# One core's two-resolution attention with a routed MLP: wider pooled-score matmuls, x tiles left uncleared, v sums in three steps, and a new order of all steps

## The chip, the cores and the metric

The kernel runs on one core of a Trainium2 chip. Its time is the device time of one execution in microseconds; the median of three runs is 284.74 us. The core's engines work side by side, each through its own queue in program order: TensorE (PE) multiplies matrices, VectorE (DVE), ScalarE (ACT) and GpSimd (POOL) do elementwise work, and SyncE (SP) issues most of the transfers. Only PE, DVE and ACT reach PSUM, where matmul results lie.

## The reference

Eight batches (`B = 8`), eight heads, 576 tokens, head size 64. Two attentions are added, and the result goes through a routed MLP:

```python
q_d = q.reshape(B, H, Sd, factor, D).mean(axis=3)      # factor 4: 144 pooled tokens; k and v alike
out_d = sm_attn(q_d, k_d, v_d)
out_up = np.repeat(out_d, factor, axis=2)
mask = np.abs(pos[:, None] - pos[None, :]) < factor     # a band of 7 keys
out_local = softmax(where(mask, scale * q @ k.T, -1e9)) @ v
x = (out_up + out_local) as (B, S, H * D)
scores = np.einsum('bsd,d->bs', x, w_gate)
for b in range(B):
    top_idx = the 128 best tokens by scores[b]
    out[b, top_idx] = x[b, top_idx] + sigmoid(scores[b, top_idx])[:, None] * (relu(x[b, top_idx] @ w1) @ w2)
```

## The kernel before, in words

The kernel writes down some 930 **steps**, each a few instructions of one engine with the tiles it reads and writes. `Plan.order` then emits them in an order that comes from a table of numbers, `PLACES`: of all steps that could go next, the one with the smallest place does. So the table fixes, for each engine, in which order its instructions stand; at run time each engine goes through its queue and waits for what an instruction needs.

Every batch b runs through the same stages, and batches overlap:

- **Loads** (SP): `T` holds q and k of the batch, transposed (2.3 MB, two tiles in turn); `raw` the four token phases of v (1.15 MB, one tile); `vw` the windows of v in three pieces. Weights come in eight pieces through `hid`; ACT and DVE split each into a high and a low fp16 half (L409, L412).
- **Pooling**: for batch 0 DVE sums q and k (L484); for the others POOL does it in two halves of the heads, each by `one` (L492, `half<-T`) and `two` (L496, `dT<-half`). POOL sums v (`add`, L450 and L452, three additions in one step) and spreads the 16 tokens beyond the 128th (`spread`, L458).
- **Coarse attention** (`coarse`): pooled scores in two groups u (L529, the 16 tokens beyond the 128th in L536), row maxima on DVE (L547), exponentials on ACT, copies for the last tokens on POOL (L570, L576, `erx`), transposes on PE (L513, L591 to L593), products with v (L603, L611, L618, L625), division on DVE (`dens`, L636 to L647). The result `ods` is raised to full length: for batches 0 and 1 by matmuls (L678, `raise_by_products`, with a POOL step `apart`, L666), for the others by 12 DMAs from `ods` and `pd` into the tile `x` (`raise_by_copies`: four steps `up` of two DMAs, one step `up_last` of three, one `down`).
- **Local attention** (`local`), three groups of two, two and one tiles: scores (mask L756, q times k L768), maximum and difference on DVE (`top`, L779 and L780), exponential on ACT, transposes (L513) and products (L814) on PE, division on DVE (`norm`, L824 to L826), the sum into `x` (`add`, L836; on DVE for batches 0 and 7, on POOL for the others), and the score of each token on DVE (`dot`, L843). Then SP stores `x` (L864, five DMAs for a batch).
- **Route**: token scores are joined (L880), transposed (L896), compared (L906), counted (L916) and turned into a one-hot matrix (ACT L935) that picks 128 tokens (`pick`, PE L943; `found`, DVE L952). POOL gathers their rows from the output (L958).
- **MoE**: transposes of the gathered rows (L981), up (L1002 to L1004) and down (L1024 to L1026) matmuls in fp16 halves, low halves on DVE (L988, L1014), the sum (`join`, DVE L1032) and a scatter by POOL (L1037).

At the start POOL clears tiles (`set_up`, L366), among them both `x` tiles of 128 by 2560 floats.

Of the kernel before, what the change touches and what calls it, by code (L numbers as in the profile page):

```python
# [21 lines left out]
P = 128  # L22
# [9 lines left out]
UL = 2  # L32
FAST = (0, 7)
SUMS = (0,)
LIFT = (0,1)
TU = [list(range(u, min(u + UL, NT))) for u in range(0, NT, UL)]
XS = 16.0
# [2 lines left out]

EARLY = {
    "load": 0.48, "pool": -1.58, "coarse": -1.53, "raise": 3.84, "local": -0.18,
    "sum": 1.35, "lift": 0.5, "route": -8.17, "moe": 3.14, "weights": 3.02,
}


PLACES = """
# [33 lines left out]
"""  # L81


# [171 lines left out]
def tile_multires_attention_moe(ctx: ExitStack, tc: tile.TileContext, qk, vw, vp, cs, w_gate, w1, w2, outs):  # L255
# [97 lines left out]
    def pref(kind, b, more=0.0):  # L353
        return b + EARLY[kind] + more
# [7 lines left out]
    )  # L362

    def set_up():
        for t in (*qzs, first, *xs):
            pool.memset(t, 0.0)  # L366
        pool.memset(ones, 1.0)
        for t in vds:
            pool.memset(t[:, :, D:], 1.0)

    step("POOL", 6000, set_up, (), ("zero",), -9)

    def set_up2():
        dve.tensor_copy(identb, ident)
# [63 lines left out]
    def load_v(b):  # L438
        raw = Buf("raw")
        step(  # L440
            "SP", 0, lambda: sp.dma_start(
            out=raw.at.rearrange("p (r s) h d -> p r (s h d)", r=2), in_=vp[b].rearrange("r p s h d -> p r (s h d)"),
        ), (), (raw,), pref("load", b, 0.35),
            moves=[(400, 3070)],
        )
        vd = vd_[b] = Buf("vd")

        def add():
            o = vd.at[:, :, :D]
            pool.tensor_tensor(out=o, in0=raw.at[:, 0], in1=raw.at[:, 1], op=ALU.add)  # L450
            for r in range(2, FACTOR):
                pool.tensor_tensor(out=o, in0=o, in1=raw.at[:, r], op=ALU.add)  # L452

        step("POOL", 4180, add, (raw, "zero"), (vd,), pref("pool", b, 0.2))
        vr = vr_[b] = Buf("vr")

        def spread():
            pool.tensor_tensor(  # L458
                out=vr.at, in0=vd.at[:, H : H + 1, :].broadcast_to([P, HH, D1]),
                in1=bk.unsqueeze(2).broadcast_to([P, HH, D1]), op=ALU.mult,  # L460
            )

        step("POOL", 610, spread, (vd, "cst"), (vr,), pref("pool", b, 0.3))
        vwin[b] = []
        for i, tiles in enumerate(TU):
            t = Buf(f"vw{i}")
            vwin[b].append(t)

            def go(t=t, tiles=tiles):
                sp.dma_start(out=t.at, in_=vw[b][:, 2 * tiles[0] : 2 * tiles[-1] + 2])  # L470

            step("SP", 0, go, (), (t,), pref("load", b, 0.4 + 0.1 * i), moves=[(350, 815 * len(tiles))])
# [44 lines left out]
    def coarse(b):  # L517
        dT, qz, vd, vr = qkdT[b], qz_[b], vd_[b], vr_[b]
        ed, er, erx, ptr = Buf("ed"), Buf("er"), Buf("erx"), Buf("ptr")
        for u in range(2):  # L520
# [3 lines left out]
            def scores(u=u, s=s):  # L524
                for i in range(2):
                    hp = 2 * u + i
                    for x in range(2):
                        for a in range(2):
                            pe.matmul(  # L529
                                s.at[64 * x : 64 * x + 64, a, SD * i : SD * (i + 1)],  # L530
                                lhsT=dT.at[64 * a : 64 * a + 64, hp, 0, 64 * x : 64 * x + 64],
                                rhs=dT.at[64 * a : 64 * a + 64, hp, 1, :], start=True, stop=True,
                            )
                if u:
                    for hp in range(HP):
                        pe.matmul(  # L536
# [63 lines left out]
        def products():  # L600
# [20 lines left out]
                        start=False, stop=True, skip_group_check=True,  # L621
                    )
            for a in range(2):
                for x in range(2):
                    pe.matmul(  # L625
                        od.at[64 * x : 64 * x + 64, a, : HH * D1],
                        lhsT=ptr.at[64 * a : 64 * a + 64, 0, 64 * x : 64 * x + 64],
                        rhs=vr.at[64 * a : 64 * a + 64].rearrange("p h d -> p (h d)"), start=False, stop=True,
                        skip_group_check=True,
                    )  # L630

        step("PE", 2280, products, (ptd, ptr, vd, vr), (od,), pr, 70)
        op = lambda: od.at[:, :, : (HH + 1) * D1].rearrange("p a (h d) -> p a h d", d=D1)
# [102 lines left out]
    def local(b):  # L736
        T, x, sc = qkT[b], xb[b], Buf("sc")
        scs[b] = sc
        for i, tiles in enumerate(TU):
# [37 lines left out]
            def top(s=s, mx=mx, ex=ex, ns=ns, ng=ng):  # L777
# [4 lines left out]
                    in1=mx.at[:, :, :ng].unsqueeze(3).broadcast_to([P, 2, ng, KW]), op=ALU.subtract,  # L782
                )

            step("DVE", 250 + 1070 * ns, top, (), (s, mx, ex), pr, 80)
            step(
                "ACT", 100 + 430 * ns,
                lambda ex=ex, ng=ng: act.activation(ex.at[:, :ng], ex.at[:, :ng], AF.Exp, scale=scale),  # L788
                (), (ex,), pr, 100,
            )  # L790
            ps, pt = Buf("pair", "local"), Buf("pt")
            pr = pref("local", b, 0.3 * i + 0.05)

# [343 lines left out]
```

## Time and profile before

| | us |
|---|---|
| median of three runs (284.70 to 285.36) | 284.74 |
| the profiled execution | 282.83 |
| its span, first to last instruction | 281.0 |
| PE busy | 230.4 |
| DVE busy | 211.6 |
| POOL busy | 164.0 |
| ACT busy | 127.9 |

Busy time counts the stretches in which an engine had work in it, so overlapping matmuls count once. The granted TensorE clock is 0.953 of full over the span.

### The profile page before, as it was taken

What the parts mean: (1) busy time and instruction counts of PE and PEld (TensorE: products, weight loads), DVE (VectorE), ACT (ScalarE), POOL (GpSimd) and SP (SyncE); (2) the same over time, 40 slices, a digit from 0 to 9 for tenths busy, and PEclk for the clock granted to TensorE, in tenths of its full rate; (3) what the DMA queues carried; (4) which work ended last, traced back from release to release, by engine and by line L of the source; (5) the groups of instructions that cost most, each with busy time, mean ns of one, the idle gap of its engine ahead of it and who ended that gap; (6) DMA issues with size and microseconds to landing.
All of it is one profiled execution on the core that took longest, in us unless ns stands there. A gap on an engine that the chain in (4) does not pass through costs nothing.

```text
span 281.0 us, 11847 instructions
## 1 busy us (share of the span) xinstructions
PE 230.4 (82%) x5160; PEld 172.9 (62%) x5160; DVE 211.6 (75%) x507; ACT 127.9 (46%) x264; POOL 164.0 (58%) x177
## 2 busy tenths in 40 slices
PE   0668767698685876689898999898999989999992
PEld 0455455555564765666686677655875776886670
DVE  4975595979999698398798897798997899862311
ACT  0476588536582475144533366236715436232010
POOL 8253999794999876909936797595633321111201
PEclk9989979979779899799999999999999999999998
DMA  7999996909899999887597879978878871521100
GB/s 277 418 354 418 413 395 228 340 8 303 249 354 290 385 355 335 231 179 185 162 394 246 251 214 326 272 178 236 184 171 229 212 186 54 145 67 37 40 37 37
DMA packets 23229, 66.00 MB, mean 235 GB/s; under 512 B 3346, under 2 KB 3346, under 8 KB 23178
## 3 DMA queue, kind: packets, MB, share of 16 engines
q1 hardware_dynamic: 21898, 61.06, 68.1%
q0 software_dynamic: 1280, 4.20, 4.5%
q8 instruction: 40, 0.66, 0.9%
q14 instruction: 11, 0.09, 0.1%
HBM read 47.02 MB, written 11.73 MB: 209 GB/s over the span
## 4 chain that ended last, share of the span: by engine, by line
PE 41%; DVE 16%; issue 15%; DMA 11%; POOL 10%; ACT 6%; SPq 1%; POOLq 0%; DVEq 0%; ACTq 0%
DMA xe<-out_dram,idx 5%; PE ps L814 4%; PE ps L1002 4%; PE ps L1004 3%; PE ps L1003 3%; PE ps L1024 3%; PE ps L513 3%; PE ps L1026 3%; PE ps L1025 3%; DVE t L843 3%; DMA T<-in_qk_dram 2%; POOL half L492 2%; DMA raw<-in_vp_dram 2%; PE ps L768 2%; PE ps L611 2%
## 5 line engine op out<-in xcount | busy, mean ns | idle before, releaser
L836 POOL TENSOR_TENSOR x<-x,t 128x512 f32<-128x512 f32 x30 | 39.2, 1315 | 19.9 <-DVE t L826 12.4
L1002 PE MATMUL ps<-xeh,w1h 128*128 128x128 f16 x256 | 45.5, 221 | 2.1 <-DVE t L843 1.5
L1003 PE MATMUL ps<-xel,w1h 128*128 128x128 f16 x256 | 45.3, 221 | 0.0
L1004 PE MATMUL ps<-xeh,w1l 128*128 128x128 f16 x256 | 45.3, 221 | 0.0
L814 PE MATMUL ps<-vw,pt 64*64 64x65 f32 x1280 | 29.0, 227 | 9.0 <-issue 7.5
L814 PEld LDWEIGHTS ps<-vw,pt 64*64 64x64 f32 x1280 | 23.9, 137 | 17.1 <-issue 11.4
L492 POOL TENSOR_TENSOR half<-T 128x1152 f32<-128x1152 f32 x14 | 29.5, 2105 | 2.6 <-DMA T<-in_qk_dram 2.3
L843 DVE SCALAR_TENSOR_TENSOR t<-x,ps 128x512 f32<-128x512 f32 x40 | 26.9, 682 | 5.1 <-PE ps L1026 1.6
L768 PE MATMUL ps<-T 64*58 64x64 f32 (+1 forms) x1280 | 26.5, 228 | 4.4 <-issue 4.4
L768 PEld LDWEIGHTS ps<-T 64*58 64x58 f32 (+1 forms) x1280 | 25.5, 138 | 6.6 <-issue 5.4
L788 ACT ACTIVATE ex<-ex 128x1024 f32<-128x1024 f32 (+1 forms) x24 | 21.9, 915 | 15.3 <-DVE ex L780 15.1
L826 DVE TENSOR_TENSOR t<-ps,den 128x512 f32<-128x512 f32 x40 | 27.7, 691 | 1.5
L779 DVE TENSOR_REDUCE mx<-ps 128x16 f32<-128x1024 f32 (+1 forms) x24 | 25.0, 1040 | 3.4 <-PE ps L768 1.9
L1003 PEld LDWEIGHTS <-w1h 128*128 128x128 f16 x256 | 25.3, 99 | 2.7 <-issue 2.0
L1002 PEld LDWEIGHTS <-w1h 128*128 128x128 f16 x256 | 25.2, 99 | 2.6 <-issue 0.7
L906 DVE SCALAR_TENSOR_TENSOR beat<-ps,scp,first 128x640 bf16<-128x640 f32 (+4 forms) x40 | 22.6, 613 | 5.6 <-PE ps L896 5.1
L1024 PE MATMUL ps<-w2h,hid 128*128 128x512 f16 x64 | 24.3, 380 | 1.9 <-DVE t L843 1.3
L800 ACT COPY pt<-ps 128x1024 f32<-128x1024 f32 (+1 forms) x24 | 20.9, 878 | 10.7 <-PE ps L513 10.3
L780 DVE TENSOR_TENSOR ex<-ps,mx 128x1024 f32<-128x1024 f32 (+1 forms) x24 | 25.1, 1047 | 0.8
L1004 PEld LDWEIGHTS <-w1l 128*128 128x128 f16 x256 | 25.3, 99 | 0.1
L1026 PE MATMUL ps<-w2h,hid 128*128 128x512 f16 x64 | 24.2, 379 | 0.0
L1025 PE MATMUL ps<-w2l,hid 128*128 128x512 f16 x64 | 24.2, 379 | 0.0
(113 smaller groups left out, 494.5 us busy)
## 6 DMA issues: line engine op xcount, KB each, us to landing
T<-in_qk_dram SPq DMA_DIRECT2D x7, 2304.0 KB
raw<-in_vp_dram SPq DMA_DIRECT2D x8, 1152.0 KB
vw<-in_vw_dram SPq DMA_DIRECT2D x16, 520.0 KB
out_dram<-x SPq DMA_DIRECT2D x14, 480.0 KB
x<-ods SPq DMA_DIRECT2D x48, 120.0 KB
hid<-in_moe_w_dram SPq DMA_DIRECT2D x8, 512.0 KB
T<-in_qk_dram SPq DMA_DIRECT2D x4, 576.0 KB
vw<-in_vw_dram SPq DMA_DIRECT2D x8, 260.0 KB
```

The source lines that it names most:

```text
L492: pool.tensor_tensor(out=hv.at, in0=e2[..., 0], in1=e2[..., 1], op=ALU.add)
L768: pe.matmul(s.at[64 * e : 64 * e + qn, a, c : c + KW], lhsT=T.at[64 * a : 64 * a + 64, hp, 0, q0s[blk] : q0s[blk] + qn], rhs=T.at[64 * a : ...
L814: pe.matmul(o.at[64 * e : 64 * e + 64, a, D1 * hp : D1 * (hp + 1)], lhsT=pt.at[64 * a : 64 * a + 64, e, HP * n + hp, :], rhs=vl.at[64 * a ...
L826: dve.tensor_tensor(out=t.at.rearrange("p (g a d) -> p a g d", a=2, d=D), in0=ov[:, :, :, 0:D], in1=den.at.unsqueeze(3).broadcast_to([P, 2 ...
L836: (dve if last else pool).tensor_tensor(out=x.at[:, j], in0=x.at[:, j], in1=t.at, op=ALU.add)
L843: dve.scalar_tensor_tensor(out=t.at, in0=x.at[:, j], scalar=1.0, in1=wg, op0=ALU.mult, op1=ALU.mult, accum_out=sc.at[:, j : j + 1],)
L1002: pe.matmul(o, lhsT=w1h[:, c, fs], rhs=xeh.at[:, c, :], start=c == 0, stop=False)
L1003: pe.matmul(o, lhsT=w1h[:, c, fs], rhs=xel.at[:, c, :], start=False, stop=False)
L1004: pe.matmul(o, lhsT=w1l[:, c, fs], rhs=xeh.at[:, c, :], start=False, stop=c == NC - 1)
L1024: pe.matmul(py.at, lhsT=hid.at[:, 0, f, :], rhs=w2h[:, f, :], start=f == 0, stop=False)
L1025: pe.matmul(py.at, lhsT=hid.at[:, 0, f, :], rhs=w2l[:, f, :], start=False, stop=False)
L1026: pe.matmul(py.at, lhsT=hid.at[:, 1, f, :], rhs=w2h[:, f, :], start=False, stop=f == NF - 1)
```

## The change

Four edits. The pooled scores and the products of the last 16 tokens run with all 128 queries as one stationary operand of 64 by 128 instead of two of 64 by 64, so there are half as many of these matmuls with as many moving columns each. The `x` tiles are no longer cleared. The three additions of v become three steps, which the order may part. `PLACES` is a new table for the 950 steps. (A second form of the local exponentials is added for batches in `EXPS`, which is empty: no step uses it. The costs written beside the steps are the planner's.)

```diff
-        for t in (*qzs, first, *xs):
+        for t in (*qzs, first):
             pool.memset(t, 0.0)
...
-        def add():
-            o = vd.at[:, :, :D]
-            pool.tensor_tensor(out=o, in0=raw.at[:, 0], in1=raw.at[:, 1], op=ALU.add)
-            for r in range(2, FACTOR):
-                pool.tensor_tensor(out=o, in0=o, in1=raw.at[:, r], op=ALU.add)
-
-        step("POOL", 4180, add, (raw, "zero"), (vd,), pref("pool", b, 0.2))
+        for r in range(1, FACTOR):
+            def add(r=r):
+                o = vd.at[:, :, :D]
+                pool.tensor_tensor(out=o, in0=o if r > 1 else raw.at[:, 0], in1=raw.at[:, r], op=ALU.add)
+
+            step("POOL", 1400, add, (raw, "zero"), (vd,), pref("pool", b, 0.2 + 0.03 * r))
...
-                    for x in range(2):
-                        for a in range(2):
-                            pe.matmul(
-                                s.at[64 * x : 64 * x + 64, a, SD * i : SD * (i + 1)],
-                                lhsT=dT.at[64 * a : 64 * a + 64, hp, 0, 64 * x : 64 * x + 64],
-                                rhs=dT.at[64 * a : 64 * a + 64, hp, 1, :], start=True, stop=True,
-                            )
+                    for a in range(2):
+                        pe.matmul(
+                            s.at[:, a, SD * i : SD * (i + 1)], lhsT=dT.at[64 * a : 64 * a + 64, hp, 0, :P],
+                            rhs=dT.at[64 * a : 64 * a + 64, hp, 1, :], start=True, stop=True,
+                        )
...
             for a in range(2):
-                for x in range(2):
-                    pe.matmul(
-                        od.at[64 * x : 64 * x + 64, a, : HH * D1],
-                        lhsT=ptr.at[64 * a : 64 * a + 64, 0, 64 * x : 64 * x + 64],
-                        rhs=vr.at[64 * a : 64 * a + 64].rearrange("p h d -> p (h d)"), start=False, stop=True,
-                        skip_group_check=True,
-                    )
+                pe.matmul(
+                    od.at[:, a, : HH * D1], lhsT=ptr.at[64 * a : 64 * a + 64, 0, :],
+                    rhs=vr.at[64 * a : 64 * a + 64].rearrange("p h d -> p (h d)"), start=False, stop=True,
+                    skip_group_check=True,
+                )
...
-    0 1 10 12 18 49 50 2 3 4 5 6 25 33 7 8 9 11 37 46 15 52 59 51 88 173 63 98 185 177 207 248 190 231 244 256 287 317
+    0 1 9 11 18 48 53 2 3 5 4 6 23 28 30 36 7 10 8 12 56 131 14 54 55 59 81 129 130 155 230 136 158 207 213 265 325
```

The table moves steps on every engine. Three places matter below. In these rows the line numbers are those of the respective kernel, and the number behind a name is that of the buffer. POOL, from the step `apart` of batch 0 on (`t<-odr`), before (`T_78`, `vd_88`, `vr_90` belong to batch 1, `T_77` to batch 2):

```order
L666 TENSOR_TENSOR t_118<-odr_103,cst 128x512
L492 TENSOR_TENSOR half_79<-T_78 128x1152
L496 TENSOR_TENSOR dT_80<-half_79 128x576
L450 TENSOR_TENSOR vd_88<-raw_86 128x9x64
L452 TENSOR_TENSOR vd_88<-vd_88,raw_86 128x9x64 x2
L492 TENSOR_TENSOR half_79<-T_78 128x1152
L496 TENSOR_TENSOR dT_80<-half_79 128x576
L458 TENSOR_TENSOR vr_90<-vd_88,cst 128x260
L492 TENSOR_TENSOR half_79<-T_77 128x1152
```

and the same place after:

```order
L662 TENSOR_TENSOR t_119<-odr_103,cst 128x512
L492 TENSOR_TENSOR half_79<-T_78 128x1152
L496 TENSOR_TENSOR dT_80<-half_79 128x576
L492 TENSOR_TENSOR half_79<-T_78 128x1152
L496 TENSOR_TENSOR dT_80<-half_79 128x576
L452 TENSOR_TENSOR vd_88<-raw_86 128x9x64
L452 TENSOR_TENSOR vd_88<-vd_88,raw_86 128x9x64 x2
L458 TENSOR_TENSOR vr_90<-vd_88,cst 128x260
L492 TENSOR_TENSOR half_79<-T_77 128x1152
```

The second half of batch 1's pooled q and k now comes ahead of its v sums instead of behind them. DVE between `dens` of batch 1 (which ends with the first row, `odr_104`) and `dens` of batch 2 (which begins with `dend_105`), before:

```order
L647 SCALAR_TENSOR_TENSOR odr_104<-ps_64,dend_106,odr_104 128x64
L836 TENSOR_TENSOR x_123<-x_123,t_119 128x512
L843 SCALAR_TENSOR_TENSOR t_119,sc_125<-x_123,ps_66 128x512
L779 TENSOR_REDUCE mx_107<-ps_63 128x16
L780 TENSOR_TENSOR ex_110<-ps_63,mx_107 128x2x8x64
L836 TENSOR_TENSOR x_123<-x_123,t_117 128x512
L843 SCALAR_TENSOR_TENSOR t_117,sc_125<-x_123,ps_66 128x512
L636 TENSOR_SCALAR dend_105<-ps_65 128x10
```

and after:

```order
L775 TENSOR_REDUCE mx_107<-ps_63 128x16
L776 TENSOR_TENSOR ex_110<-ps_63,mx_107 128x2x8x64
L837 TENSOR_SCALAR den_121<-ps_65 128x8
L838 RECIPROCAL den_121<-den_121 128x8
L839 TENSOR_TENSOR t_117<-ps_65,den_121 128x2x4x64
L849 TENSOR_TENSOR x_123<-x_123,t_116 128x512
L856 SCALAR_TENSOR_TENSOR t_116,sc_125<-x_123,ps_66 128x512
L775 TENSOR_REDUCE mx_108<-ps_63 128x16
L776 TENSOR_TENSOR ex_111<-ps_63,mx_108 128x2x8x64
L632 TENSOR_SCALAR dend_105<-ps_64 128x10
```

A third division of batch 1 (`den_121`) and the second `top` of batch 2 (`mx_108`, `ex_111`) now stand ahead of `dens` of batch 2. SP near the end, where `x_123` is batch 6 and `x_124` batch 7, before:

```order
L707 DMA x_124<-ods_102 60x1x512 x8
L470 DMA vw_85<-in_vw_dram 128x520
L707 DMA x_124<-ods_102 48x1x512
L707 DMA x_124<-pd_157 12x1x512
L707 DMA x_124<-pd_157 56x1x512
L864 DMA out_dram<-x_123 48x5x512
L864 DMA out_dram<-x_123 10x5x512
L864 DMA out_dram<-x_123 48x5x512
L864 DMA out_dram<-x_123 6x5x512
L864 DMA out_dram<-x_123 4x4x512
```

and after:

```order
L703 DMA x_124<-ods_102 60x1x512 x2
L877 DMA out_dram<-x_123 48x5x512
L877 DMA out_dram<-x_123 10x5x512
L877 DMA out_dram<-x_123 48x5x512
L877 DMA out_dram<-x_123 6x5x512
L877 DMA out_dram<-x_123 4x4x512
L703 DMA x_124<-ods_102 48x1x512
L703 DMA x_124<-pd_157 12x1x512
L703 DMA x_124<-pd_157 56x1x512
L703 DMA x_124<-ods_102 60x1x512 x2
```

The last five copies into batch 7's `x` have moved behind the five stores of batch 6.

## Rows read from the trace of the kernel before

**Rows 1.** Page, part 1: busy us (share of span) xinstructions of each engine.

```profile
PE 230.4 (82%) x5160; PEld 172.9 (62%) x5160; DVE 211.6 (75%) x507; ACT 127.9 (46%) x264; POOL 164.0 (58%) x177
```

**Rows 2.** Windows: stretch and length, busy us (instructions) by engine, granted clock, DMA share, GB/s.

```profile
0.00:45.00 45.00, 28.03 (x739) 20.48 (x741) 31.39 (x50) 25.18 (x47) 29.90 (x31) 0.92 0.93 359
45.00:100.00 55.00, 41.99 (x1104) 31.29 (x1104) 46.42 (x106) 30.57 (x63) 45.45 (x43) 0.88 0.84 283
...
130.00:200.00 70.00, 64.34 (x1545) 48.45 (x1536) 59.12 (x162) 32.31 (x73) 50.14 (x56) 1.00 0.82 249
200.00:275.00 75.00, 71.87 (x1250) 53.81 (x1248) 50.69 (x135) 25.47 (x51) 17.63 (x29) 1.00 0.46 118
```

**Rows 3.** Timeline of PE: start, us, engine, line, operation, tiles, tile shape, count.

```profile
60.50 0.67 PE L625 MATMUL ps<-vr,ptr 64*64 64x260 f32 x8
...
63.22 0.72 PE L529 MATMUL ps<-dT 64*64 64x144 f32 x16
...
65.29 0.72 PE L513 MATMUL ps<-cst,ex 64*128 64x64 f32 x16 [0.66 <-ACT pt L800]
...
68.01 0.70 PE L814 MATMUL ps<-vw,pt 64*64 64x65 f32 x32
```

**Rows 4.** Timeline of POOL, the start; in brackets idle time before and its releaser.

```profile
1.59 4.68 POOL L366 MEMSET x<- 128x2560 f32 x2
...
12.31 1.40 POOL L450 TENSOR_TENSOR vd<-raw 128x576 f32<-128x576 f32 x1 [5.92 <-DMA raw<-in_vp_dram]
```

**Rows 5.** Timeline of POOL, 26 to 47 us.

```profile
26.04 1.95 POOL L666 TENSOR_TENSOR t<-odr,cst 128x512 f32<-128x512 f32 x1 [4.66 <-DVE odr L647]
...
32.72 2.72 POOL L452 TENSOR_TENSOR vd<-vd,raw 128x576 f32<-128x576 f32 x2
...
37.58 1.14 POOL L496 TENSOR_TENSOR dT<-half 128x576 f32<-128x576 f32 x1
...
39.27 2.11 POOL L492 TENSOR_TENSOR half<-T 128x1152 f32<-128x1152 f32 x1
...
46.41 0.29 POOL L576 COPY erx<-ed 128x128 f32<-128x128 f32 x1
```

**Rows 6.** Timeline of DVE and PE, waits between 30 and 62 us.

```profile
32.19 0.76 DVE L547 TENSOR_REDUCE mxd<-ps 128x4 f32<-128x576 f32 x1 [3.02 <-PE ps L529]
...
55.80 0.30 PE L591 MATMUL ps<-cst,erx 128*128 128x128 f32 x1 [2.71 <-DVE t L843]
...
61.24 0.17 DVE L636 TENSOR_SCALAR dend<-ps 128x10 f32<-128x10 f32 x1 [1.78 <-PE ps L625]
```

**Rows 7.** Groups of DVE by form: count, busy us, mean ns, idle before.

```profile
L826 DVE TENSOR_TENSOR t<-ps,den 128x512 f32<-128x512 f32 x40 | 27.7, 691 | 1.5
L843 DVE SCALAR_TENSOR_TENSOR t<-x,ps 128x512 f32<-128x512 f32 x40 | 26.9, 682 | 5.1 <-PE ps L1026 1.6 <-ACT hid L1011 0.7 <-ACT xeh L985 0.6
L780 DVE TENSOR_TENSOR ex<-ps,mx 128x1024 f32<-128x1024 f32 x16 | 19.6, 1225 | 0.5
L779 DVE TENSOR_REDUCE mx<-ps 128x16 f32<-128x1024 f32 x16 | 19.5, 1219 | 1.7 <-ACT er L561 0.9 <-PE ps L768 0.8
L836 DVE TENSOR_TENSOR x<-x,t 128x512 f32<-128x512 f32 x10 | 7.7, 767 | 0.0
L412 DVE SCALAR_TENSOR_TENSOR w1l<-hid,w1h 128x1024 f16<-128x1024 f32 x4 | 4.9, 1217 | 0.0
```

**Rows 8.** Chain that ended last: batch 0's gather, start and us until landing.

```profile
82.58 12.65 DMA xe<-out_dram,idx
```

**Rows 9.** Chain (a copy into x) and timelines of SP, DVE, PE, late program.

```profile
129.76 4.75 DMA x<-ods
...
201.80 6.53 SPq L864 DMA_DIRECT2D out_dram<-x  x5
...
245.81 0.17 DVE L880 TENSOR_TENSOR scp<-sc,cst 128x5 f32<-128x5 f32 x1
...
254.04 0.27 PE L943 MATMUL ps<-va,oh 128*128 128x5 bf16 x5
```

More of the change, by code (lines that the diff above doesn't have):

```diff
@@ L34 @@
 SUMS = (0,)
+EXPS = ()
 LIFT = (0,1)
@@ L42 @@
     "load": 0.48, "pool": -1.58, "coarse": -1.53, "raise": 3.84, "local": -0.18,
-    "sum": 1.35, "lift": 0.5, "route": -8.17, "moe": 3.14, "weights": 3.02,
+    "sum": 1.35, "lift": .5, "route": -8.17, "moe": 3.14, "weights": 3.02,
 }
 PLACES = """
[33 rows of a table removed]
[33 rows of a table added]
 """
@@ L369, in set_up @@
             pool.memset(t[:, :, D:], 1.0)
-    step("POOL", 6000, set_up, (), ("zero",), -9)
+    step("POOL", 1500, set_up, (), ("zero",), -9)
     def set_up2():
@@ L461, in spread @@
             )
-        step("POOL", 610, spread, (vd, "cst"), (vr,), pref("pool", b, 0.3))
+        step("POOL", 610, spread, (vd, "cst"), (vr,), pref("pool", b, 0.32))
         vwin[b] = []
@@ L783, in top, with peak, exps @@
                 )
[L785 to L790, printed above, removed]
+            def peak(s=s, mx=mx, ns=ns, ng=ng):
+                sv = s.at[:, :, : 256 * ns].rearrange("p a (g c) -> p a g c", c=KW)
+                dve.tensor_reduce(out=mx.at[:, :, :ng], in_=sv, axis=AX.X, op=ALU.max)
+            def exps(s=s, mx=mx, ex=ex, ng=ng):
+                act.activation(mx.at[:, :, :ng], mx.at[:, :, :ng], AF.Copy, scale=-scale)
+                for a in range(2):
+                    for g in range(ng):
+                        act.activation(
+                            ex.at[:, g, KW * a : KW * (a + 1)], s.at[:, a, KW * g : KW * (g + 1)], AF.Exp,
+                            bias=mx.at[:, a, g : g + 1], scale=scale,
+                        )
+            if b in EXPS:
+                step("DVE", 130 + 530 * ns, peak, (), (s, mx), pr, 80)
+                step("ACT", 200 + 1650 * ns, exps, (), (s, mx, ex), pr, 100)
+            else:
+                step("DVE", 250 + 1070 * ns, top, (), (s, mx, ex), pr, 80)
+                step(
+                    "ACT", 100 + 430 * ns,
+                    lambda ex=ex, ng=ng: act.activation(ex.at[:, :ng], ex.at[:, :ng], AF.Exp, scale=scale),
+                    (), (ex,), pr, 100,
+                )
             ps, pt = Buf("pair", "local"), Buf("pt")
```

64 rows, old and new, of the table PLACES are left out of this document.

## The prediction

> **What bounds the kernel now.** I read the page's busy shares first: PE 82%, DVE 75% [rows 1]. Such a share is a mean over stages, so I took the table of windows next [rows 2]. In it the program has two halves. From 130 to 200 us PE is busy 64.3 of 70 us, from 200 to 275 us 71.9 of 75: there PE sets the pace, and no order of steps can win much. Up to 100 us it is busy 28.0 of 45 and 42.0 of 55 us: 30 us idle. DVE is idle 13.6 us of the first 45 and 8.6 of the next 55. So what a new order can win lies in the first 100 us: work that fills those holes no longer has to be done later. Third I read the timelines of POOL, DVE and PE there for what ends the holes. From 26 us on POOL works through the pooling of batches 1 and 2 [rows 5], DVE waits 3.02 us for pooled scores that need it, and before `dens` of batch 2 DVE waits 1.78 us for the products while PE had waited 2.71 us for DVE [rows 6]: engines that wait on each other in turn, with none full.
>
> **The x tiles left uncleared** take 4.68 us of POOL away [rows 4]. Behind them POOL waits 5.92 us for `raw`, which is on its way since the start, so the v sums begin at 12.31 us as before. Value 0; the cover is that transfer, and were it gone the edit would be worth the 4.68 us.
>
> **The wider matmuls.** A pooled-score group was 16 records of 64x64 with 144 columns in 0.72 us, the products of the last tokens 8 records with 260 columns in 0.67 us [rows 3]. Each gets half the records, twice as wide. The nearest rows for what width costs: 16 records of 64x128 with 64 columns take 0.72 us, 32 of 64x64 with 65 columns 0.70 us [rows 3]. Half as many, twice as wide: the same time. So I take 0 for PE. The end below zero is that a record costs the same whatever its width: half of 0.72 for the 16 groups and half of 0.67 for the 8 is 5.8 + 2.7 = 8.5 us at most, and less by the fixed latency in each; I put 4.6 (some 0.23 and 0.12 us a group). Above zero I see nothing, since the 64x128 row already pays for the width. The Trainium skill (TensorEngine Tiling (Array Packing), Instruction Overhead) states about 60 cycles of overhead for each matmul on trn2, the same latency for 1 column as for 60. By that, 160 records fewer at 2.4 GHz would be an estimate of 4 us less on PE. The trace disagrees so far: 32 records in 0.70 us leave 22 ns for each, work included [rows 3]. It is a rival below.
>
> **The v sums as three steps** are the same instructions (two take 2.72 us [rows 5]); by themselves 0. They let POOL turn to something else between two sums, up to 2.7 us sooner.
>
> **The new order.** POOL first: from `apart` of batch 0, which nothing moves (26.04 + 1.95 = 28.0 us), batch 1's two halves now follow at once, 2 x (2.11 + 1.14) = 6.5 us, so its pooled q and k are complete at 34.5 us instead of 37.58 + 1.14 = 38.7 [rows 5]: 4.2 us sooner. Its v sums end 0.6 us later than the old second half did, at about 39.3 with the spread, and still ahead of the `erx` copies, which stood at 46.41 and now stand one addition (1.1 us) sooner. Batch 1's scores, maxima and exponentials so come into the DVE hole of 3.02 us and the ones after it.
>
> DVE second, the term that carries the forecast. I compared the sets of steps ahead of `dens` of batch 2. Nothing has left; seven steps have come: three divisions of batch 1, 3 x 0.69 = 2.1 us; the second `top` of batch 2, 1.22 + 1.23 = 2.4; one weight half, 1.2; one `add` and one `dot` of batch 0, 0.8 + 0.7 [rows 7]. That is 7.2 us. They fit: up to 45 us alone DVE has 13.6 us of holes [rows 2].
> When does `dens` of batch 2 come? It began at 61.24 [rows 6]. POOL now has a half, its sum and another half of batch 3 ahead of batch 2's `erx` copies, 2.11 + 1.14 + 2.11 = 5.4 us [rows 5]. Those copies had been done by about 53 us (46.41, 0.7 for both copies, three sums 4.1, spread and copies 1.6), while PE took them at 55.80, held by DVE [rows 6]. So 2.8 us of the 5.4 were slack, and 2.6 are late; 1.1 us of that comes back from the addition that moved behind batch 1's copies. Delay 0 to 2.6 us, I take 1.2. The lead is 7.2 - 1.2 = **6.0 us**, bounds 4.6 and 7.2.
>
> Does PE follow? Ahead of the products of batch 2 it has three more product groups of 0.70 us [rows 3], two score groups, a transposition, and one lift in another's place, about 4 us; it was idle 13.0 us between 45 and 100 [rows 2], so it can.
> Is the lead kept? Up to `pick` of batch 3 (in the middle of the stretch from 130 us on) both programs have the same amount of DVE work ahead, to within half a microsecond, and the same of PE; only which differs (three MoE steps and a count of batch 4 in place of scores of batch 5). From there PE sets the pace in either. So a lead there reaches the end.
> At the end, after `pick` of batch 7 at 254.04 [rows 9], four down steps fewer are left than before, but they are done ahead of it on a full PE: 0, at best 2.6 us.
>
> **Sum.** Profiled execution 282.83 (span 281.0 and 1.8 around it): 282.8 - 0 - 0 - 6.0 = 276.8. The median of the runs lies 1.9 above the profiled execution, so in its terms 284.7 - 6.0 = **278.7**.
>
> **Rivals.**
> *Given back at the first gather.* Batch 0's gather took 12.65 us until its rows were there [rows 8], with transfers all around it. Its `found` has the moved steps ahead of it, so it comes no sooner; but up to the first MoE step of DVE both orders have nearly the same work, so between the two DVE now has some 7 us less to do. If the gather takes as long again, DVE and PE stand still for what they had won, and 0 to 1.5 us stay: 283.2 to 284.7, I say 284.0. For it: the row. Against: SP issues batch 4's `T` sooner now, since its tile is free when the local scores of batch 2 are through, and those stand further ahead.
> *Records cost, not width.* PE shorter by 4.6 us in all; on the path lie the groups behind 130 us, five of 16 and three of 8, 5 x 0.23 + 3 x 0.12 = 1.5 us, up to all 4.6: 278.7 - 4.6 to 278.7 - 1.5, 274.1 to 277.2.
> *The other side: batch 7's copies.* SP now issues batch 6's stores ahead of the last five copies into batch 7's `x`. The stores wait for POOL's last `add` of batch 6 (1.3 us), take 6.53 us to issue, the five copies at no more than a store's 1.3 us each 4 to 6.5 (I take 4), the landing 4.75 [rows 9]: 16.6 us. From the division that feeds that `add` to the `add` of batch 7 that needs the copies DVE has about 19 us of steps; these two `add` and `dot` pairs are its last ahead of the joined score (245.81 before [rows 9]). So 2.4 us of slack: from there every microsecond is paid in full, since 35 us of dependent work follow. If the stores wait for free slots as long again as they take to issue (6.5 us) and the copies likewise (4), the end is 8 us late and eats the lead: 284.7 - 6.0 + 8.1 = 286.8.
> *The order does not do what it says*: the steps pulled ahead wait in turn for PE, which runs at 0.88 to 0.92 of its clock there [rows 2], and a third of the lead stays: 282.5.
>
> **How the numbers follow.** Forecast 278.7 (277.5 to 281): 0.50. Given back: 0.17, half of it within 0.3%. Records: 0.12. Copies late: 0.13. Order empty: 0.08. Faster by over 0.3%, about what a measurement can tell from no change (below 283.9): 0.50 + 0.12 + 0.08 + 0.07 = 0.77; within: 0.10; slower: 0.13. The range 274.0 to 286.0 leaves out the upper end of the copies and the lower end of the records, less than 0.2.
>
> **What would show it.** No MEMSET of `x`, and POOL's first v sum still at about 12.3 us behind a longer wait for `raw`. A score group of 8 records still near 0.7 us. The second `two` of batch 1 ending at 34 to 35 us; `dens` of batch 2 at 61 to 64 with 4 us or more less idle time on DVE up to there; the joined score of batch 7 near 240. I am wrong if DVE idles between `found` of batch 0 and its first MoE step, if SP sits long at the stores of batch 6, or if score groups shrink to 0.5 us.

## The result: 1.3% slower, and the profile after

The changed kernel's runs have a median of 288.95 us (288.41 to 293.31), those of the kernel before on the same chip 285.05 (284.70 to 285.91). Ratio 1.013, interval 1.009 to 1.017: slower, where I had forecast 0.979. Ratios here are of undisturbed runs; a median given without a ratio has all runs in it. The profiled execution took 288.46, its span 286.7.

The page, part 1, and the four windows answer to [rows 1, 2]:

```profile
PE 231.8 (81%) x5000; PEld 172.7 (60%) x5000; DVE 216.2 (75%) x507; ACT 126.9 (44%) x264; POOL 158.0 (55%) x175
```

```profile
0.00:45.00 45.00, 28.08 (x677) 21.80 (x678) 31.90 (x51) 20.85 (x39) 23.46 (x29) 0.92 0.90 342
45.00:100.00 55.00, 43.21 (x1061) 30.75 (x1061) 49.19 (x103) 33.73 (x71) 43.35 (x39) 0.91 0.83 273
130.00:200.00 70.00, 63.60 (x1337) 48.30 (x1327) 57.29 (x163) 30.68 (x70) 51.90 (x58) 0.98 0.85 268
200.00:275.00 75.00, 67.69 (x1376) 51.24 (x1374) 51.66 (x126) 28.03 (x58) 15.94 (x24) 1.00 0.46 109
```

Two things stand out. DVE has the same 507 instructions and is busy 4.6 us longer. And in the last window, where I had PE setting the pace, PE is busy 67.7 instead of 71.9 of 75 us: it waits there.

Where the time went is seen by two points that both programs pass: the one-hot matmul `pick` of batch 3, ahead of which both have about the same amount of work, and that of batch 7. PE's timeline of the changed kernel, and DVE's for the last `join`:

```profile
161.63 0.28 PE L956 MATMUL ps<-va,oh 128*128 128x5 bf16 x5
...
256.78 0.27 PE L956 MATMUL ps<-va,oh 128*128 128x5 bf16 x5
...
281.44 0.75 DVE L1045 SCALAR_TENSOR_TENSOR xe<-ps,gs,xe 128x512 f32<-128x512 f32 x1 [4.14 <-PE ps L1039]
```

| profiled execution, us | up to `pick` b3 | `pick` b3 to `pick` b7 | `pick` b7 to last `join` |
|---|---|---|---|
| before | 164.4 | 89.6 | 21.7 |
| after | 161.6 | 95.2 | 24.7 |

So a lead of 2.8 us is there in the middle, not 6.0; then 5.6 are lost, and 3.0 in the tail. Three questions: why the lead is small, what the middle loses, what the tail loses.

**The tail** answers first. Rows of PE, ACT and DVE from the transposes of batch 7's rows (L994) on; L1037 to L1039 are the three matmuls of a down step:

```profile
264.61 0.60 PE L994 MATMUL ps<-cst,xe 128*128 128x128 f32 x4
...
265.48 0.38 PE L1039 MATMUL ps<-w2h,hid 128*128 128x512 f16 x1
...
265.89 0.60 ACT L998 ACTIVATE xeh<-ps 128x512 f16<-128x512 f32 x1 [3.73 <-PE ps L1039]
266.54 0.38 PE L1037 MATMUL ps<-w2h,hid 128*128 128x512 f16 x1 [0.69 <-ACT xeh L998]
...
267.46 0.69 DVE L1001 SCALAR_TENSOR_TENSOR xel<-ps,xeh 128x512 f16<-128x512 f32 x1 [4.56 <-PE ps L1039]
268.20 0.38 PE L1037 MATMUL ps<-w2h,hid 128*128 128x512 f16 x1 [0.85 <-DVE xel L1001]
...
275.70 0.38 PE L1037 MATMUL ps<-w2h,hid 128*128 128x512 f16 x1 [0.69 <-ACT hid L1024]
...
277.36 0.38 PE L1037 MATMUL ps<-w2h,hid 128*128 128x512 f16 x1 [0.85 <-DVE hid L1027]
```

These waits make no sense as data: down matmuls of batch 6 (266.54) take nothing from `xeh` of batch 7, and `xeh`, which reads the transposes, waits for a down matmul (265.48). What the two have in common is a PSUM tile. The kernel's PSUM tiles are two banks wide (`ps_63` to `ps_66`); the transposes lie in bank 3, batch 6's down sums in bank 2. Read from the two programs: in both tails PE has nearly the same steps in the same order, but before, the transposes are in bank 4 and batch 7's down sums in bank 3, in tiles in which nothing else runs beside them. The theory is then: **the waits treat the two banks of a tile as one**, and which step lands beside which is decided by the order.

**The start.** DVE and POOL, 50 to 71 us:

```profile
50.37 4.35 DVE L413 SCALAR_TENSOR_TENSOR w1l<-hid,w1h 128x1024 f16<-128x1024 f32 x2
...
56.40 2.46 DVE L849 TENSOR_TENSOR x<-x,t 128x512 f32<-128x512 f32 x1
...
70.19 0.17 DVE L632 TENSOR_SCALAR dend<-ps 128x10 f32<-128x10 f32 x1 [0.68 <-PE ps L622]
```

```profile
50.06 3.57 POOL L452 TENSOR_TENSOR vd<-vd,raw 128x576 f32<-128x576 f32 x2
53.71 1.48 POOL L458 TENSOR_TENSOR vr<-vd,cst 128x260 f32<-128x260 f32 x1
56.21 2.11 POOL L492 TENSOR_TENSOR half<-T 128x1152 f32<-128x1152 f32 x1 [1.02 <-DMA T<-in_qk_dram]
```

An addition that takes 0.68 us alone takes 2.46, a low weight half 2.2 instead of 1.22 [rows 7], and POOL's two sums 3.57 instead of 2.72 [rows 5], its spread 1.48 instead of 0.62, where they meet: the addition at 56.40 begins 0.2 us behind POOL's `half` and ends 0.5 us after it. `dens` of batch 2 starts at 70.19, not at 61 to 64. DVE's busy time up to `dens` of batch 2, before and after (windows of DVE alone):

```profile
0.00:61.24 61.24, 43.20 (x74) 0.92 0.86 327
```

```profile
0.00:70.19 70.19, 55.34 (x88) 0.93 0.84 309
```

12.1 us more, where the seven steps that came were priced at 7.2.

### The profile page after: what moved, and what is told of

It reads as the page before. It is cut to its first block, busy times and chain, and to the rows that moved or that the text cites. A ratio compares the mean times of both kernels' runs of the same rounds, so it can differ in the third digit from the quotient of the medians.

```text
span 286.7 us, 11514 instructions
## 1 busy us (share of the span) xinstructions
PE 231.8 (81%) x5000; PEld 172.7 (60%) x5000; DVE 216.2 (75%) x507; ACT 126.9 (44%) x264; POOL 158.0 (55%) x175
## 5 line engine op out<-in xcount | busy, mean ns | idle before, releaser
L1015 PE MATMUL ps<-xeh,w1h 128*128 128x128 f16 x256 | 44.9, 220 | 4.0 <-DVE hid L1027 1.3
L849 POOL TENSOR_TENSOR x<-x,t 128x512 f32<-128x512 f32 x30 | 37.7, 1273 | 13.8 <-DVE den L837 10.7
L1017 PE MATMUL ps<-xeh,w1l 128*128 128x128 f16 x256 | 44.7, 220 | 0.0
L492 POOL TENSOR_TENSOR half<-T 128x1152 f32<-128x1152 f32 x14 | 30.4, 2173 | 10.5 <-DMA T<-in_qk_dram 10.0
L764 PE MATMUL ps<-T 64*58 64x64 f32 (+1 forms) x1280 | 27.3, 233 | 5.3 <-issue 5.3
L1037 PE MATMUL ps<-w2h,hid 128*128 128x512 f16 x64 | 24.3, 379 | 8.3 <-DVE t L856 2.7
L1024 ACT ACTIVATE hid<-ps 128x512 f16<-128x512 f32 x16 | 9.4, 595 | 37.3 <-PE ps L1017 22.9
L1050 POOL DMA_INDIRECT out_dram<-xe,idx x8 | 8.1, 1009 | 32.2 <-DVE xe L1045 28.1
L528 PE MATMUL ps<-dT 64*128 64x144 f32 x128 | 14.4, 349 | 12.8 <-DVE dT L484 8.6
```

Source lines behind the costliest of these rows:

```text
L492: pool.tensor_tensor(out=hv.at, in0=e2[..., 0], in1=e2[..., 1], op=ALU.add)
L764: pe.matmul(s.at[64 * e : 64 * e + qn, a, c : c + KW], lhsT=T.at[64 * a : 64 * a + 64, hp, 0, q0s[blk] : q0s[blk] + qn], rhs=T.at[64 * a : ...
L849: (dve if last else pool).tensor_tensor(out=x.at[:, j], in0=x.at[:, j], in1=t.at, op=ALU.add)
L1015: pe.matmul(o, lhsT=w1h[:, c, fs], rhs=xeh.at[:, c, :], start=c == 0, stop=False)
L1017: pe.matmul(o, lhsT=w1l[:, c, fs], rhs=xeh.at[:, c, :], start=False, stop=c == NC - 1)
L1037: pe.matmul(py.at, lhsT=hid.at[:, 0, f, :], rhs=w2h[:, f, :], start=f == 0, stop=False)
```

## The experiments

**Edits or order.** e1 is the changed code in the order of before, e2 the code of before in the new order (only `PLACES` differs).

> The three edits of the code (wider matmuls, x not cleared, v sums in three steps) in the order of the kernel before; the three v sums stand one behind another where the one step stood. Theory 'order': all of the loss of 3.9 us is the table's, so this runs as the kernel before, 285 us (284 to 286). Rival 'edits': the edits cost the time themselves, 288 to 290 us.

> The code of the kernel before (narrow matmuls, x cleared, one v step) with the new table; the one v step takes the place of the last of the three. Theory 'order': 288 to 290 us, as the changed kernel. Rival 'edits': 285 us, as before. If the new order needs the freed GpSimd (a v step of 4.1 us at a stretch), 290 us or more.

e1: median 286.14 (281.64 to 287.07) beside 286.27 (282.79 to 292.35) for before on the same chip. e2: ratio 1.016 (1.003 to 1.030). The loss is the order's; what the three edits are worth by themselves is too small for these scattered runs to show, which agrees with the forecast of 0.

**Halves of the two orders.** The new order up to `pick` of batch 3 and then the old one (e3), and the reverse (e4); `PLACES` only.

> The changed kernel's code; new order up to the one-hot matmul of batch 3 (pick), then the old order. At that point the new order was 2.8 us ahead of the old one in the traces, and lost 5.6 us from there to pick of batch 7 and 2.9 behind it. Theory 'late loss' (the loss lies in the new order's second half): 285.0 - 2.8 = 282 us (281 to 284). Rival 'bad start' (the early new order leaves a state, in transfers and tiles, that costs time later whatever follows): 286 to 290 us.

> The changed kernel's code; old order up to pick of batch 3, then the new order. Theory 'late loss': 285.0 + 5.6 + 2.9 = 293 us (290 to 294). Rival 'bad start': 283 to 286 us.

Both theories missed: 1.056 (1.042 to 1.070) and 1.058 (1.033 to 1.083). Both programs lose time behind the seam. In e3 the window there has PE busy 50.65 of 70 us at a granted clock of 0.78 (columns as in [rows 2]):

```profile
130.00:200.00 70.00, 50.65 (x1027) 39.84 (x1018) 40.81 (x109) 25.84 (x58) 41.82 (x46) 0.78 0.72 228
```

These two orders could not be cut in two and their halves priced apart; nothing follows on where the lead went.

**Two buffers of the tail exchanged.** e5 gives the changed kernel's tail the banks of before, e6 the tail of before the banks of after. The order stays.

```diff
+SEATS = {178: (4,), 181: (3,)}        # e6: {178: (3,), 181: (4,)}
...
         if buf.banks:
...
+            seat = SEATS.get(self.taken + sum(1 for b, _ in taken if b.banks))
+            if seat:
+                return max(banks[i][0] for i in seat), seat
```

> The changed kernel with two PSUM buffers of the tail exchanged: the transposes of batch 7's gathered rows go to bank 4 instead of 3, batch 7's down sums to bank 3 instead of 4; same order. In the changed kernel these share a two-bank tile with work that runs beside them (down sums of batch 6 in bank 2, second up half of batch 7 in bank 5), and PE then waits for ACT and DVE between down matmuls (0.69, 0.85, 0.69, 0.85 us in the trace, 3.9 and 6.9 us for what takes 2.7 and 5.0 before). Theory 'shared tile' (two banks of one tile are treated as one by the waits): 3 us faster than the changed kernel, 285.5 to 286.5 where it takes 289, and the four waits are gone. Rival 'true need' (PE would wait for that data anyway): unchanged, 288.5 to 289.5.

> The kernel before with the same two buffers of the tail put where the changed kernel has them (transposes of batch 7 in bank 3, its down sums in bank 4); same order, same code otherwise. Theory 'shared tile': 3 us slower than before, 287.5 to 288.5 where before takes 285, with the four waits of 0.7 to 0.9 us in the tail. Rival 'true need': as before, 284.5 to 285.5.

e5: 0.999 of before (0.993 to 1.006), where after has 1.013: 3.8 us back. e6: 1.019 (1.011 to 1.026): 5 us lost by the ratio, 3.3 by the medians; its tail in the trace is 25.4 us instead of 21.7. The tail of e5 (21.0 us; lines of its code stand 7 lower), with the transposes at L1001:

```profile
263.49 0.60 PE L1001 MATMUL ps<-cst,xe 128*128 128x128 f32 x4
263.93 0.38 PE L1044 MATMUL ps<-w2h,hid 128*128 128x512 f16 x1
264.12 0.60 ACT L1005 ACTIVATE xeh<-ps 128x512 f16<-128x512 f32 x1 [3.08 <-PE ps L1001]
...
264.57 0.38 PE L1044 MATMUL ps<-w2h,hid 128*128 128x512 f16 x1
264.75 0.69 DVE L1008 SCALAR_TENSOR_TENSOR xel<-ps,xeh 128x512 f16<-128x512 f32 x1 [2.98 <-ACT xeh L1005]
```

Down matmuls follow each other without a wait, and `xeh` waits for what it reads. e6 has the waits that before had not:

```profile
262.59 0.38 PE L1031 MATMUL ps<-w2h,hid 128*128 128x512 f16 x1 [0.69 <-ACT xeh L992]
...
264.25 0.38 PE L1031 MATMUL ps<-w2h,hid 128*128 128x512 f16 x1 [0.85 <-DVE xel L995]
```

That settles it for the tail: two buffers' places, nothing else, make and unmake the loss.

**The gate vector in a tile of its own.** Each token score (`dot`) reads the gate vector in PSUM, the second bank of the fourth tile; matmuls run in the first. e7 is this edit in after, e8 in before.

```diff
-    psum = [ppool.tile([P, 2, 512], F32, name=f"ps{i}") for i in range(4)]
+    psum = [ppool.tile([P, 2 if i < 3 else 1, 512], F32, name=f"ps{i}") for i in range(4)]
...
-    wg = psum[3][:, 1]
+    wg = ppool.tile([P, 512], F32, name="wg")
```

> The changed kernel with the gate vector, which every token score reads out of PSUM, in a tile of its own; until now it shared the fourth tile with bank 6, in which matmuls run. Theory 'shared tile': the waits of PE for the token score (down <- t, four of them, 2.7 us, transposes <- t 2.2 us) and of the token score for PE are gone; of some 6 us of such waits on PE, DVE and ACT a half or more lies on the path: 283 to 287 us where the changed kernel takes 289. Rival 'true need': 288.5 to 289.5.

> The kernel before with the gate vector in a tile of its own. Theory 'shared tile': the 2.71 us wait of PE for the token score, three of the token score for down sums (1.6 us) and PE's 1.5 us go; 280 to 283 us where before takes 285. Rival 'true need': 284.5 to 285.5.

e8: 0.983 (0.977 to 0.989). e7: 1.011 (1.007 to 1.016), no clear change against after's 1.013, where 2 to 6 us had been expected, although its middle stretch fell from 95.2 to 92.9 us. The waits (who waits for whom: us, times, longest) between `dot` and PE in before:

```profile
PE ps L591 <- DVE t L843: 2.7, 1, 2.7
...
DVE t L843 <- PE ps L1026: 1.6, 3, 0.9
...
PE ps L1002 <- DVE t L843: 1.5, 1, 1.5
...
PE ps L1024 <- DVE t L843: 1.3, 2, 0.9
```

and in after:

```profile
PE ps L1037 <- DVE t L856: 2.7, 4, 1.0
...
ACT xeh L998 <- DVE t L856: 2.1, 2, 1.9
...
DVE t L856 <- PE ps L1039: 1.4, 2, 0.9
```

In e7 and e8 none of these six is left. The wait of 2.71 us that I quoted in [rows 6] as "PE had waited for DVE" was one of them: transposes in bank 6 waiting for a score that only shared their tile.

**Other banks for the rest, same orders.** e9 is after once more, as a measure; e10 moves 102 of the 182 PSUM buffers, e11 the gate vector and 108, e12 the same in before (75). The edit is e5's, with a list of 182 places.

> The changed kernel itself once more, on the chip of the next three, as their measure: 288 to 289 us where before takes 285 (1.013 of it).

> The changed kernel, same order of every step, with other PSUM banks for 102 of its 182 buffers, chosen so that fewer buffers that share a two-bank tile are in use beside each other. Theory 'shared tile' (the middle's loss of some 6 us is made of the same false waits as the tail's): 281 to 284 us where the changed kernel takes 289, and the stretch from the one-hot matmul of batch 3 to that of batch 7, 95 us, is 91 or less. Rival 'order' (the middle is lost by the order itself: data that come late, the gather of batch 6 behind stores and copies): only the tail's 3 us come back, 285 to 286, and the stretch stays at 94 to 96.

> The changed kernel, same order, with the gate vector in a tile of its own and other banks for 108 of 182 buffers. Theory 'shared tile': nearly all false waits are gone; 277 to 281 us, faster than the kernel before, and the stretch from the one-hot matmul of batch 3 to that of batch 7 takes 88 to 90 us. Rival 'order': 284 to 286 us.

> The kernel before, same order, with the gate vector in a tile of its own and other banks for 75 of 182 buffers. The gate's tile alone gave 0.983 of before's time; few other false waits are left in it, so theory 'shared tile': 0.978 to 0.984 of before, 278 to 280 us. It also tells what the two orders are worth against each other once the false waits are out of both: with the lead of 2.8 us that the new order has at the one-hot matmul of batch 3, the changed kernel without false waits would be 1 to 3 us faster than this one; if the new order is no better by itself, they are level or this one is faster.

e9 1.007 (1.000 to 1.014), e10 0.999 (0.992 to 1.006), e11 **0.978** (0.970 to 0.987), e12 0.990 (0.981 to 1.000). e11 runs the new order at 2.2% less than before, better than both kernels. e10 missed the 281 to 284 us of the theory and came out at the rival's time: beside e9 its tail is 5.5 us shorter and its middle 2.5, but its stretch up to `pick` of batch 3 is 5.8 longer, so other banks can cost as well. The stretches, worked out from the starts of `pick` and `join` as above (e15 and e16, below, are e8 and e11 once more):

| profiled execution, us | up to `pick` b3 | to `pick` b7 | to last `join` |
|---|---|---|---|
| e9, after | 161.4 | 95.2 | 24.7 |
| e5, after, two buffers | 160.6 | 95.1 | 21.0 |
| e7, after, gate | 159.4 | 92.9 | 24.7 |
| e10, after, banks | 167.2 | 92.7 | 19.2 |
| e11, after, banks and gate | 163.4 | 90.9 | 19.2 |
| e16, the same | 162.0 | 91.0 | 19.2 |
| e6, before, two buffers | 165.4 | 87.3 | 25.4 |
| e8, before, gate | 163.8 | 84.5 | 21.7 |
| e15, the same | 166.8 | 87.2 | 21.7 |
| e12, before, banks and gate | 166.1 | 89.4 | 21.8 |

e12 missed its 0.978 to 0.984 and is no better than e8, so my choice of banks is not the best for that order. Single stretches are to be read with care: the middle of e6 is that of before, buffer for buffer, and took 87.3 instead of 89.6, and e8 and e15, one kernel, differ there by 2.7 us.

**The collisions of the start.** e13 is e7, e14 is e8, with the second operand of the early additions and of the low weight halves taken from PSUM; what these two kernels leave out is the true second operand (the product `t`, the high half). Waits change with it: a low half no longer waits for ACT's high half (0.3 us in after), and the first one of e14 waits 4.0 us for the gate vector.

```diff
-                        out=x.at[:, j], in0=x.at[:, j], in1=t.at, op=ALU.add
+                        out=x.at[:, j], in0=x.at[:, j], in1=t.at if b else wg, op=ALU.add
...
-    out=lo[:, cs_, :], in0=flat(), scalar=WS, in1=hi[:, cs_, :],
+    out=lo[:, cs_, :], in0=flat(), scalar=WS, in1=wg.unsqueeze(1).broadcast_to([P, 2, 512]),
```

> The changed kernel with the gate vector in its own tile (e7), and in it the five additions of batch 0 and the eight low weight halves of DVE take their second operand from the gate vector in PSUM instead of from SBUF; same shapes, same order on each engine (the sums and low halves are then not those of the reference). Theory 'collision' (DVE instructions with both operands in SBUF stretch beside GpSimd, and GpSimd with them): the early additions take 0.7 us each instead of 0.8 to 2.3, the halves 1.2 instead of 2.1 and 2.3, some 6 us of DVE less up to the division of batch 2, which starts at 62 to 65 us instead of 68.5; the end 2 to 5 us earlier than e7, ratio to before 0.994 to 1.004. Rival 'held up' (PE and ACT set that start): DVE idles instead, the start stays at 67 to 69 and the ratio at 1.008 to 1.014.

> Control: the same edit of the additions of batch 0 and the low halves in the kernel before with the gate vector in its own tile (e8). There only one addition (1.5 us) and one half met GpSimd, so theory 'collision' expects at most 1.5 us: division of batch 2 at 59 to 61 us as in e8 (60.6), ratio to before 0.978 to 0.984. If the edit gives time for another reason than the collisions, 4 us or more here too.

> e8 again, as the measure for e14 and e16: 0.98 to 0.985 of before.

> e11 again beside e15, both orders without most false waits. e11 had 0.978, e8 0.983. Theory 'lead lost to shared tiles': the new order is then the better one, by 1 to 3 us. Rival 'the new order has no lead': within 1 us of each other, or e15 ahead.

e13: 0.994 (0.988 to 0.999) against e7's 1.011, 5 us. e14: 0.974 (0.963 to 0.985) against 0.986 for e15 and 0.983 for e8: 2.6 to 3.3 us (the intervals of e14 and these two overlap), more than the 1.5 that I allowed; later low halves met POOL too (in e8 two of them took 6.28 us together). e13's DVE and its window up to `dens` of batch 2 (the profiled execution took 286.94 us where the median is 284.83, so only its rows up to there are used):

```profile
48.39 2.34 DVE L413 SCALAR_TENSOR_TENSOR w1l<-hid,wg 128x1024 f16<-128x1024 f32 x2
52.78 0.68 DVE L849 TENSOR_TENSOR x<-x,wg 128x512 f32<-128x512 f32 x1
```

```profile
0.00:67.10 67.10, 49.08 (x88) 0.92 0.90 329
```

The collisions are gone with the second SBUF operand, and DVE is busy 49.1 us up to `dens` where e7 was 54.7. But `dens` starts at 67.1, not at 62 to 65 (e7 68.5): of 5.7 us won DVE idles 4.3. The end gained; the point that I had made its measure moved by 1.4 us only. e15 and e16: 0.986 (0.971 to 1.000) and 0.981 (0.971 to 0.991); the new order is ahead by 1.3 us in the ratio and 3.4 in the medians, and the intervals overlap, so that it is the better one is not shown.

**The rest of the late start.** e17 is e16 with two weight halves of ACT moved behind batch 2's exponentials (`PLACES`), e18 that and e13's edit.

> e16 (changed kernel, gate vector in its own tile, other banks) with the two high weight halves that ACT had ahead of batch 2's second coarse exponentials put directly behind them; all other engines' orders as they were. Theory 'weights on ACT' (their transfer and 2.1 us of ACT hold the exponentials, the copies of the last tokens on GpSimd and so the products): division of batch 2 at 67 to 69 us instead of 70.5, since DVE's collisions still hold its maxima; end 0 to 2 us earlier, ratio to before 0.975 to 0.981. Rival 'maxima alone' (DVE's late maxima set it): 70 to 71 us.

> e17 and in it e13's edit: the additions of batch 0 and the low weight halves take their second operand from the gate vector in PSUM (sums and low halves are then not those of the reference). With both causes gone the division of batch 2 should begin at 62 to 65 us, as the prediction had it, and the end come some 5 us before e16's: ratio to before 0.960 to 0.968. If it stays at 66 or later, something else holds it, and that stays open.

e17: 0.988 (0.982 to 0.994), `dens` of batch 2 at 70.5 as in e16: ACT's weights were not it. e18: 0.980 (0.963 to 0.997), `dens` at 71.7. Both missed the earlier end that was expected. In e18 PE stops inside a group of products, with no wait that the profile shows (lines 21 lower):

```profile
59.27 0.51 PE L848 MATMUL ps<-vw,pt 64*64 64x65 f32 x19
63.24 0.45 PE L848 MATMUL ps<-vw,pt 64*64 64x65 f32 x13 [3.46 <-issue]
```

Less this stop the start would be near 68 (71.7 - 3.5, an estimate), still late. What else holds `dens` of batch 2 stays open.

## Why the prediction was wrong, step by step

**Right: the edits.** The first v sum still waits for `raw`, 11.89 us instead of 5.92 (it starts at 13.66, 1.3 us later than I said, because `raw` came later). Score groups of 8 records take 0.76 us, where 16 took 0.72 [rows 3]; the last tokens' products 0.71 for 4 records, 0.67 for 8. Half as many records, each twice as wide, saved nothing: the rival "records cost" falls, and with it, for this shape, what the prediction had worked out from the Trainium skill (TensorEngine Tiling (Array Packing), Instruction Overhead), that half as many matmuls would be cheaper. e1 agrees with the sum of 0.

```profile
54.87 0.71 PE L622 MATMUL ps<-vr,ptr 64*128 64x260 f32 x4
...
58.05 0.76 PE L528 MATMUL ps<-dT 64*128 64x144 f32 x8 [1.71 <-ACT ed L559]
```

**Right in direction: POOL first.** The second half of batch 1 starts its `two` at 34.7 us (37.6 before) and ends it at 35.8, where I had it complete at 34.5.

**Wrong: the DVE term, 7.2 - 1.2 = 6.0.** The seven steps were priced by means over the whole program [rows 7], but they were moved beside POOL's sums, where an addition took up to 2.46 us and a low half 2.2. Up to `dens` the additions took 4.3 us more than before and the low halves 3.1, where 0.8 and 1.2 had been priced. And a division is three instructions, of which the term counts the last: the other two, 0.15 and 0.20 us, add 1.1 for three divisions. Busy time rose by 12.1 us, not 7.2, and idle time fell by 3.2 (18.04 to 14.85), not 6.0. (Less, on the other side: a conversion at the start, L378 of before, took 2.14 us beside POOL's clearing of `x` [rows 4] and takes 0.16 now.) The delay that I took as 1.2 (bounds 0 and 2.6) was 9.0, and the lead at `pick` of batch 3 was 2.8. By the ratios of e13 (against e7) and e14 the collisions weigh some 2 us more in the new order than in the old, a difference within the runs' intervals; what else holds `dens` back stays open. The Trainium skill (SBUF — State Buffer, SBUF: two separate sides) states the rule that I left out: a DVE instruction with two SBUF inputs and a GpSimd one that reads SBUF exclude each other for a whole instruction. The rows agree, 0.68 against 2.46 us, and 0.68 again in e13 with one input in PSUM. [Rows 7] held a hint: its 767 ns for an addition was the mean of nine at 0.68 us and one at 1.53, beside POOL.

**Wrong: "PE sets the pace, so a lead reaches the end", and "tail 0, at best 2.6".** PE was taken for full because it was busy 64 of 70 us; but part of what held the engines was waits between banks of one tile, and those depend on the order. In the tail they cost 3.7 us (e5) to 5.5 (24.7 to 19.2 in e11; e5 still has PE waiting 0.69 and 0.78 us ahead of up steps of batch 6 for readers of the neighbour bank, e11 has not). Without them the tail is 2.5 us shorter than that of before: the four steps that I had at "best 2.6" (by the two programs five down steps fewer and one up step more) are there, and the waits ate them twice over. In the middle other banks and the gate's tile gave the new order 4.3 us back (95.2 to 90.9, e11); in the old one the gate's tile gave 2.4 to 5.1 (e15, e8), but e6, without it, has 87.3 too.

Of the 5.6 us that the middle lost, some 2.6 are the down steps done early. The other 3 I could not place. PE's windows tell their kind: idle 6.0 us in the middle of before, 9.7 in e9, 6.3 in e11, at a granted clock of 1.00 in all three. The longest stop of the new order is one of 2.15 us ahead of local products at 181.57 (2.16 in e7 and 2.15 in e9, where the trace names DVE's `ex` as releaser; it read the two banks that these products take next, so this wait is a true one). Behind it the clock in the profiled execution of after fell to 0.50, 1.2 GHz, from 183 to 186 us, and a product group of 0.70 us took 1.15; but e9 kept 1.00 there and needed the same 95.2. With gate and banks moved in both orders the middles differ by 1.5 us (e11, e12), with the gate's tile in both and the banks moved in the new one alone by 3.9 (e16, e15): whether the new order costs anything there beyond its 2.6 us of work is open.

**The sum by measured terms**, in spans (281.0 to 286.7): lead 2.8 instead of 6.0; middle 2.6 for the moved steps and 3.0 not placed; tail -2.5 and 5.5 for false waits: -2.8 + 5.6 + 3.0 = 5.8, against 5.7. The joined score of batch 7 came at 248.5, where I had it near 240.

**The rivals.** Given back at the first gather: no; batch 0's rows come as fast (gather at 90.1, transposes at 99.9, 9.8 us against 12.65), and DVE's longest wait in between is 0.69 us. Batch 7's copies: no; the stores of batch 6 hold SP 6.6 us as assumed, but the additions of batch 7 wait for no transfer. The order does not do what it says: in part. None of my rivals had the cause, and none of the three signs by which I wanted to know that I was wrong appeared: I looked for waits on data, and what the runs could name of the loss were collisions of DVE with POOL and waits on a neighbour.

## What to carry to other kernels

Before an order is priced, ask of each moved step which PSUM tile it will share and with whom; a wait of an engine on a step whose data it does not use, and whose banks it does not take over, is the sign of such a neighbour, and moving one buffer tests it (e5). An own tile for a value that is read all the time (e8: 1.7%) can be worth more than the order. A duration from a grouped row holds for the neighbourhood in which it was measured: for DVE instructions with two SBUF operands look at what POOL does at the new place. A lead in the middle of a program is a forecast for the middle only.

## What the runs showed of the hardware

DVE additions of 128x512 with both operands in SBUF took 0.68 us alone and up to 2.46 beside POOL, low halves of 128x1024 1.22 and up to 4.95, and POOL's pair of sums 2.71 and 3.57; with one operand in PSUM the same additions took 0.68 to 0.69 each time and the low halves 1.21 to 1.22 (e13, e14). Matmuls into one bank of a two-bank PSUM tile waited for ACT and DVE to finish with the other bank (0.69 and 0.85 us, four times in the tail of after), and did not once the buffers lay in different tiles (e5). Half as many matmuls, twice as wide, took as long (8 in 0.76 us, 16 in 0.72). PE paused for 1.7 (e13) and 3.5 us (e18) within one group of matmuls that waits for nothing shown; transfers of the two instruction queues fall into both pauses (e13 has 50 of their packets over its 285 us), but that they are the cause was not tried.
